# Output projection of the first ten token tiles in 64-row tiles, in pairs, between the transposed score tiles

## The chip, the cores and the metric

One core of a Trainium2 chip runs the whole program. The metric is the device time of one execution in microseconds (us). The engines are TensorE (PE, with its weight loads written PEld), VectorE (DVE), ScalarE (ACT), GpSimd (POOL) and SyncE (SP), which here only issues DMAs.

## What is computed

The input is x, 2048 tokens by 512 features, in float32. After a layer norm there are two branches: attention with 32 heads of 16 features, and a dense layer with GELU; the result joins them.

```python
xn = _layernorm(x)
q, k, v = (xn @ wqkv) split into 32 heads of 16
p = softmax(q @ k.T * 16 ** -0.5)
s = (p @ v) @ wo
g = silu(gelu(xn @ w1 + b1) @ w2 + b2)
out = x + s * g
```

The kernel keeps float32 accuracy by splitting each operand of a projection into a high and a low part in the PE's float32r format, and adding three products: high by high, high by low, low by high.

## The kernel before

**The stages.** The first 480 us hold the layer norm, the projections, the dense branch (its result g goes to DRAM, `g_d`) and part of the row maxima of the scores. Then comes the attention loop (lines 944 to 962): 513 steps, sixteen for each of 32 units. A unit `u` is four heads by 512 queries (`g, c = divmod(u, NCH)`); a step is one unit with one tile of 128 keys.

**A step.** `ORDER` (line 40) writes out the order of the work of one step on PE:

- T, four times (`t_one`, line 715): a transposed score tile, 128 keys by 512 queries, of one head. The contraction has 50 rows, which lie from row 0 or from row 64 of the array: `t_one(ua, ka, i % 2, 1 - i // 2)` gives the four T the row halves 1, 1, 0, 0. ACT takes the exponential of the tile into `PT` (line 724). Its four PSUM banks (`t_tile`) are used in turn, so each T waits for the exponential of the T four before it.
- S, X and Y (`s_op`, line 205): scores for the row maxima of later units, with 48 rows from row 0 or 64. DVE reduces each 128x512 tile (line 185). X and Y write the two halves of one bank from the two row halves of the array, one after the other: a no-op on POOL (line 217) waits for X, and Y waits for the no-op. Steps up to 491 have S, X and Y (`"TXSTTSTYV"`), later ones don't (`"TTTTV"`).
- V (`pv_step`, line 781): the product of the exponentials of the step before with the values, for four heads at once, in tiles of 128 rows by 32 columns.

After the sixteenth V of a unit, its sums are moved out of PSUM and divided by their denominators (`o_move`, `o_den`, `o_div`), through DRAM, to give `ot`.

**What hangs between them.** `at(n, f, ..., pos=i)` (line 897) puts a piece of other work into step n behind its T number i; without `pos` behind the last T, ahead of V. All engines take their work in this program order. For a token tile t (128 tokens), the output projection consists of

- `load_gx`: two DMAs on SP, g and x of the tile into `GX[t]`;
- `w_token` (`w_round`, line 850): ACT copies the tile's attention output into the high parts `oh`, POOL subtracts to get the low parts `ol`;
- `gate`: ACT takes a tanh, DVE multiplies, which makes silu(g) up to a factor;
- `w_mul`: per k (a block of 128 features, of four) three matmuls with 128 rows and 512 columns into one PSUM bank (`s_tile`, a ring of three banks);
- `w_out`: DVE multiplies the bank by the gate (`w_gate`, line 883), POOL adds x (line 888), SP writes it out (line 889).

Tiles 0 to 9 (`NW`) are dealt out from step 492 (`DONE`) on, one in two steps: two k in the first of them, two in the second, each time behind the fourth T:

```python
    for t in range(NW):
        n = DONE + 2 * t
        at(n - 4, load_gx, t)
        at(n - 2, w_token, t)
        at(n, w_mul, t, KS[:2])
        at(n, gate, t)
        at(n + 1, w_mul, t, KS[2:])
        at(n + 1, w_out, t, nc.gpsimd)
```

The other six tiles follow behind the loop (lines 963 to 985), as the last unit allows.

**A buffer.** The scratch tiles `gx`, `oh` and `ol` are rings of 4, 3 and 3 buffers. `home(KB)` is the place of the keys `kt0`, which are no longer used by then.

Of the kernel before, what the change touches and what calls it, by code (L numbers as in the profile page):

```python
# [8 lines left out]
F32 = mybir.dt.float32  # L9
F32R = mybir.dt.float32r  # L10
# [6 lines left out]
P = 128  # L17
S = 2048
D = 512
H = 32  # L20
DH = 16
KT = D // P
# [11 lines left out]
NW = 10  # L34
# [7 lines left out]
KB = 3  # L42
# [5 lines left out]
def fused(ctx: ExitStack, tc: tile.TileContext, x, wqk, wv, wo, w1, b1, w2, b2, out):  # L48
    nc = tc.nc
# [26 lines left out]
    def mm3(ps, lhs, rhs, first, last, then=None):  # L76
        n = 0
        for a, b in ((0, 0), (0, 1), (1, 0)):
            nc.tensor.matmul(ps, lhs[a], rhs[b], start=first and n == 0, stop=last and n == 2)  # L79
            n += 1  # L80
            if then:
                then()

    QS, QT, MX, NM, MH = {}, {}, {}, {}, {}
    SYNC = mybir.DependencyInfo(mybir.DependencyClass.Sync, mybir.DependencyReason.DATA)
# [5 lines left out]
    def s_tile(held=False):  # L91
        pool = s_ring.pop(0)
        if not held:
            s_ring.append(pool)
        return pool.tile([P, CH], F32, name="ps"), pool
# [29 lines left out]
    def slot(i, shape, dtype=F32):  # L125
        return big.tile(list(shape), dtype, name=f"slot{i}")
# [27 lines left out]
    done = {u: 0 for u in range(NU)}  # L154
# [148 lines left out]
    for j in range(len(pairs)):  # L303
        for h in range(2):
# [9 lines left out]
            n = 2 if nd < len(parts) and parts[nd][2] and ready - nd > room else 1  # L314
            n = max(n, need - 2 * (left - 1))
            while nd < ready and n > 0:
                c, f, k = parts[nd]
# [224 lines left out]
    s_when, put, row = [], [0], [0, 0]  # L542
# [217 lines left out]
    wb = ctx.enter_context(tc.tile_pool(name="work_b", bufs=2))  # L760
# [4 lines left out]
    wo_h = kp.tile([P, KT, D], F32R, name="wo_h")  # L765
    wo_l = kp.tile([P, KT, D], F32R, name="wo_l")

    WR = {}

    def load_wo(k):  # L770
        WR[k] = wb.tile([P, 2, D], F32, name="gx", bufs=4)[:, 0]
        nc.sync.dma_start(WR[k], wo[k * P:(k + 1) * P, :])

    def wo_high(k):
# [51 lines left out]
    GX, OTS, PW, homes = {}, {}, {}, {}  # L826

    def home(i):
        if i not in homes:
            homes[i] = (slot(i, (P, KT, D)) if i < KB else  # L830
                        keep_r.tile([P, 2 * KT, D], F32, name="kt0"))
        return homes[i]

    def load_gx(t):
        i = 2 * (t % NCH)
        if t < NW:
            GX[t] = wb.tile([P, 2, D], F32, name="gx", bufs=4)
        elif t < NT - NCH:
            GX[t] = home(KB)[:, i:i + 2]
        else:  # L840
            GX[t] = home(1 + i // KT)[:, i % KT:i % KT + 2]
        nc.sync.dma_start(GX[t][:, 0], g_d[t * P:(t + 1) * P, :])
        nc.sync.dma_start(GX[t][:, 1], x[t * P:(t + 1) * P, :])
# [4 lines left out]
        nc.vector.scalar_tensor_tensor(g, e, 1.0, g, op0=OP.add, op1=OP.mult)  # L848

    def w_round(blocks, src, lo):  # L850
        oh = wb.tile([P, KT, P], F32R, name="oh", bufs=3)
        ol = wb.tile([P, KT, P], F32R, name="ol", bufs=3)
        n = len(blocks)
        nc.scalar.activation(oh[:, :n], src, AF.Copy)
        lo.tensor_sub(ol[:, :n], src, oh[:, :n].bitcast(F32))
        for i, b in enumerate(blocks):
            OTS[b] = (oh[:, i], ol[:, i])

    def w_token(t):
        c, i = divmod(t, NCH)  # L860
        w_round([(t, k) for k in KS], ot[c][:, :, i * P:(i + 1) * P], nc.gpsimd)

    def w_chunk(k, lo):
        w_round([(t, k) for t in T3], ot[NCH - 1][:, k].rearrange("p (t s) -> p t s", s=P), lo)

    def cols(t):
        n = 2 if t == NT - 1 else 1
        return [slice(i * D // n, (i + 1) * D // n) for i in range(n)]

    def w_mul(t, ks, parts=(0, 1)):  # L870
        if t not in PW:
            PW[t] = [ps_t.tile([P, CH], F32, name="pst") if NW <= t < NT - NCH or i else
                     ps_m.tile([P, CH], F32, name="ps") if t == NT - 1 else s_tile()[0]
                     for i, cs in enumerate(cols(t))]
        for i, cs in enumerate(cols(t)):
            if i in parts:
                for k in ks:
                    mm3(PW[t][i][:, :cs.stop - cs.start], OTS[t, k], (wo_h[:, k, cs], wo_l[:, k, cs]),
                        k == 0, k == KT - 1)

    def w_gate(t, i=0):
        gx, cs = GX[t], cols(t)[i]
        nc.vector.scalar_tensor_tensor(gx[:, 0, cs], PW[t][i][:, :cs.stop - cs.start], 0.5, gx[:, 0, cs],
                                       op0=OP.mult, op1=OP.mult)
# [12 lines left out]
    def at(n, f, *a, pos=3):  # L897
        todo.setdefault((n, pos), []).append((f, a))

    KS = tuple(range(KT))  # L900
# [21 lines left out]
            at(16 * u + (31 if u < NU - 2 else 22), o_div, u, nc.gpsimd)  # L922
    T3 = range(NT - NCH, NT)
    late = range(NW, NT)
    for t in range(NW):
        n = DONE + 2 * t
        at(n - 4, load_gx, t)
        at(n - 2, w_token, t)
        at(n, w_mul, t, KS[:2])
        at(n, gate, t)  # L930
        at(n + 1, w_mul, t, KS[2:])
        at(n + 1, w_out, t, nc.gpsimd)
    for i, t in enumerate(late):
        n = L - 2 * len(late) - 1 + 2 * i
        at(n - 4, load_gx, t)
        at(n, gate, t)
    for i, t in enumerate(late[:2]):
        at(L - 2 + i, w_token, t)
    for k in range(KT):
        at(104 + 16 * k, load_wo, k)  # L940
        at(110 + 16 * k, wo_high, k)
        at(114 + 16 * k, wo_low, k)
    jobs.extend(heads[made[0]:])
    for n in range(L + 1):
        ua, ka = divmod(n, 16)
        want = due(n) - due(n - 1)
        i = 0
        for op in ORDER[want] if n > 1 else ("TTTTV", "TTSTSVT")[n]:
# [8 lines left out]
            else:  # L957
# [4 lines left out]
                i += 1  # L962
    o_move(NU - 1)
    w_mul(late[0], KS)
    w_chunk(0, nc.gpsimd)
    o_den(NU - 1)
# [52 lines left out]
```

## Time and profile before

| what | value |
|---|---|
| time, median of 3 runs | 1606.27 us (1606.13 to 1606.79) |
| profiled execution, span from first to last instruction | 1603.9 us |
| profiled execution, own time | not told apart from its span by the profile |
| PE busy | 1593.1 us (99%) |
| DVE busy | 1383.5 us (86%) |
| ACT busy | 1260.5 us (79%) |
| POOL busy | 377.5 us (24%) |
| mean granted PE clock | 1.000 |

The profile is of one execution. In a timeline each row gives the start in us from the span's start, the length, the engine, the line of the kernel, the operation, what it writes and reads, and how many were merged; in brackets how long the engine was idle before it and for whom it waited. A PE row's length holds the passage through the array: matmuls overlap, so the distance of their starts tells what one costs. "128*32 128x512" is a matmul with weights of 128 rows and 32 columns and a moving operand of 128 rows and 512 columns.

### The profile page before, as it was taken

The numbers are of one execution on the slowest core, as the hardware profiler recorded it, in microseconds if no ns is written. First come the engines' busy times: TensorE is split into PE (matmuls) and PEld (weight loads), VectorE is DVE, ScalarE is ACT, GpSimd is POOL, SyncE is SP. The second block draws the span as 40 slices with busy tenths as digits, with TensorE's granted clock in tenths as the row PEclk, the third lists the DMA queues.
The fourth block names the chain that finished last, engine by engine and source line by source line (L and its number), as shares of the span: only waits on it lengthen the run. The fifth ranks groups of instructions, "written<-read, shape, count | busy, mean of one in ns | idle before, by whom it ended". The sixth has DMA issues, their size and how long they took to land.

```text
span 1603.9 us, 32476 instructions
## 1 busy us (share of the span) xinstructions
PE 1593.1 (99%) x12146; PEld 915.7 (57%) x12146; DVE 1383.5 (86%) x2267; ACT 1260.5 (79%) x2524; POOL 377.5 (24%) x398
## 2 busy tenths in 40 slices
PE   8999999999999999999999999999999999999998
PEld 7899989999994444444444444444444444444445
DVE  7489888888989999999999999999999999999734
ACT  4333443434339999999999999999999999999984
POOL 4145565766640001011100200100010000000144
PEclk9999999999999999999999999999999999999999
DMA  6525343454322113111410411221141111110152
GB/s 204 149 59 151 116 136 97 148 145 126 114 89 70 40 30 70 29 36 42 79 32 27 68 42 29 59 42 29 30 70 30 30 29 37 34 29 22 58 200 91
DMA packets 76798, 116.93 MB, mean 73 GB/s; under 512 B 25156, under 2 KB 26436, under 8 KB 75464
## 3 DMA queue, kind: packets, MB, share of 16 engines
q1 hardware_dynamic: 73180, 102.42, 22.4%
q0 software_dynamic: 3264, 12.35, 3.9%
q8 instruction: 96, 1.57, 0.4%
q14 instruction: 62, 0.51, 0.1%
q10 hardware_dynamic: 196, 0.07, 0.0%
HBM read 84.35 MB, written 25.97 MB: 69 GB/s over the span
## 4 chain that ended last, share of the span: by engine, by line
PE 97%; DVE 1%; ACT 0%; DMA 0%; issue 0%; SPq 0%; DVEq 0%; ACTq 0%
PE pv L787 32%; PE ps L179 18%; PE pst L722 16%; PE ps L573 12%; PE pst L573 7%; PE ps L722 5%; PE ps L79 3%; PE pv L573 2%; PE pst L79 1%; DVE slot L74 0%; DMA xt<-in_x 0%; PE pst L259 0%; DVE st L407 0%; PE ps L259 0%; DVE xn L421 0%
## 5 line engine op out<-in xcount | busy, mean ns | idle before, releaser
L185 DVE TENSOR_REDUCE mx<-ps 128x2 f32<-128x512 f32 x2048 | 1299.4, 685 | 153.3 <-PE ps L179 84.9
L724 ACT ACTIVATE slot<-pst 128x512 f32<-128x512 f32 x1533 | 835.1, 612 | 14.2 <-PE pst L722 4.1
L787 PE MATMUL pv<-slot,vsb 128*32 128x512 f32 x4096 | 545.3, 605 | 0.0
L179 PE MATMUL ps<-kt,slot 48*128 48x512 f32 (+1 forms) x1364 | 393.1, 376 | 0.0
L722 PE MATMUL pst<-qt,kt 50*128 50x512 f32 x1149 | 378.1, 430 | 0.5 <-DVE gt L655 0.3
L722 PEld LDWEIGHTS pst<-qt,kt 50*128 50x128 f32 x1149 | 183.0, 184 | 249.6 <-ACT slot L724 246.2
L724 ACT ACTIVATE slot<-ps 128x512 f32<-128x512 f32 x515 | 314.8, 612 | 12.9 <-PE pst L722 8.2
L179 PEld LDWEIGHTS ps<-kt,slot 48*128 48x128 f32 x1364 | 211.3, 184 | 34.2 <-DVE mx L185 23.3
L573 PE MATMUL ps<-slot,w1h 64*128 64x512 f32 x1088 | 220.5, 394 | 0.0
L179 PE MATMUL ps<-kt,qz 48*128 48x512 f32 x512 | 214.9, 420 | 0.0
L179 PE MATMUL ps<-slot,slot 48*128 48x512 f32 (+1 forms) x598 | 172.6, 376 | 0.0
L722 PE MATMUL ps<-qt,kt 50*128 50x512 f32 x387 | 163.0, 423 | 0.0
L573 PEld LDWEIGHTS ps<-slot,w1h 64*128 64x128 f32 x1088 | 152.9, 185 | 6.8 <-ACT junk L587 0.8
L787 PEld LDWEIGHTS pv<-slot,vsb 128*32 128x32 f32 x4096 | 80.6, 108 | 119.8 <-issue 112.0
L573 PE MATMUL ps<-slot,w1l 64*128 64x512 f32 x544 | 143.0, 392 | 0.0
L367 POOL TENSOR_TENSOR hl<-hg,hh 128x512 fp32r<-128x512 f32 x76 | 96.8, 1296 | 131.7 <-ACT hh L366 95.0
L722 PE MATMUL pst<-qt,slot 50*128 50x512 f32 x384 | 119.8, 424 | 0.0
L587 ACT ACTIVATE junk<-ident_r 1x1 f32<-1x1 f32 x92 | 18.0, 196 | 126.4 <-PE pst L573 123.2
L722 PEld LDWEIGHTS ps<-qt,kt 50*128 50x128 f32 x387 | 71.1, 184 | 69.4 <-ACT slot L724 56.5
L179 PEld LDWEIGHTS ps<-kt,qz 48*128 48x128 f32 x512 | 93.7, 183 | 17.4 <-DVE mx L185 0.6
L243 POOL CAST nmh<-nm 128x16 fp32r<-128x16 f32 x32 | 6.3, 197 | 413.1 <-PE pst L722 209.1
L722 PEld LDWEIGHTS pst<-qt,slot 50*128 50x128 f32 x384 | 61.5, 184 | 71.9 <-ACT slot L724 71.6
(150 smaller groups left out, 1744.9 us busy)
## 6 DMA issues: line engine op xcount, KB each, us to landing
raw<-in_w SPq DMA_DIRECT2D x88, 256.0 KB
qk_h<-hh SPq DMA_DIRECT2D x32, 256.0 KB
qk_l<-hl SPq DMA_DIRECT2D x32, 256.0 KB
qt<-qk_h SPq DMA_DIRECT2D x128, 64.0 KB
slot<-qk_h SPq DMA_DIRECT2D x92, 64.0 KB
xt<-in_x SPq DMA_DIRECT2D x16, 256.0 KB
g_d<-gt POOLq DMA_DIRECT2D x16, 256.0 KB, 3.1
qt<-qk_l SPq DMA_DIRECT2D x64, 64.0 KB
```

Of the source, the lines that this page charges most:

```text
L79: nc.tensor.matmul(ps, lhs[a], rhs[b], start=first and n == 0, stop=last and n == 2)
L179: return nc.tensor.matmul(ps[:, c0:c0 + w], QS[u][r, p, qi * P:(qi + 1) * P], kts[u // NCH % KB][p][r, k0:k0 + w], start=True, stop=True).ins
L185: nc.vector.tensor_reduce(MX[u][:, 2 * p:2 * p + 2, qi, ki][:, heads, parts], ps.rearrange("p (n c) -> p n c", c=HC), axis=AX.X, op=OP.max)
L243: nc.gpsimd.tensor_copy(hl[:, 0], nm)
L367: nc.gpsimd.tensor_sub(hl, raw, hh.bitcast(F32))
L573: i = nc.tensor.matmul(ps, lhs[r], rhs[r], start=first, stop=last).ins
L587: i = nc.scalar.activation(junk[:, :1], ident_r[:1, :1].bitcast(F32), AF.Copy).ins
L722: nc.tensor.matmul(ps, kts[g % KB][p][r, k * P:(k + 1) * P], QT[u][r, p, :], start=True, stop=True)
L724: nc.scalar.activation(PT[u, k][:, 2 * p + a, :], ps, AF.Exp, scale=SCALE)
L787: nc.tensor.matmul(PV[u][32 * j:32 * j + 32, :], vsb[:, k, h:h + 32], PT[u, k][:, j, :], start=(k == 0), stop=(k == NT - 1))
```

## The change

Tiles 0 to 9 are now taken in pairs (t, t + 1), each pair in four steps. Each 128-row matmul becomes two of 64 rows. In the first two steps of a pair, tile t takes rows 0 to 63 of all four k and tile t + 1 rows 64 to 127; in the last two the tiles swap row halves (`side`). Per step and pair there are twelve 64-row matmuls, alternating between row half 0 and 1: four each behind the first, the second and the third T. A no-op on POOL waits for the last matmul ahead of the swap, and the first two behind it wait for the no-op. `w_out` of both tiles stands in the pair's last step. Tile t + 1's `w_token` moves to the first T of the step before the pair; the loads stand three and two steps ahead of the pair. The ring of `gx` has three buffers and those of `oh` and `ol` four; tiles 3 and 7 use the place of `kt0`.

```diff
     def load_wo(k):
-        WR[k] = wb.tile([P, 2, D], F32, name="gx", bufs=4)[:, 0]
+        WR[k] = wb.tile([P, 2, D], F32, name="gx", bufs=3)[:, 0]
...
-        if t < NW:
-            GX[t] = wb.tile([P, 2, D], F32, name="gx", bufs=4)
+        if t < NW and i < 6:
+            GX[t] = wb.tile([P, 2, D], F32, name="gx", bufs=3)
         elif t < NT - NCH:
-            GX[t] = home(KB)[:, i:i + 2]
+            GX[t] = home(KB)[:, i - 6 * (t < NW):][:, :2]
...
-        oh = wb.tile([P, KT, P], F32R, name="oh", bufs=3)
-        ol = wb.tile([P, KT, P], F32R, name="ol", bufs=3)
+        oh = wb.tile([P, KT, P], F32R, name="oh", bufs=4)
+        ol = wb.tile([P, KT, P], F32R, name="ol", bufs=4)
...
+    turned = {}
+
+    def w_half(t, part, third):
+        two = (t, t + 1)
+        if part == 0 and third == 0:
+            for b in two:
+                PW[b] = [s_tile()[0]]
+        side, ks = divmod(part, 2)
+        ops = [(k, i, j) for k in KS[2 * ks:2 * ks + 2] for i, j in ((0, 0), (0, 1), (1, 0))]
+        for n in (2 * third, 2 * third + 1):
+            for a in range(2):
+                b, r, (k, i, j) = two[a ^ side], slice(64 * a, 64 * a + 64), ops[n]
+                op = nc.tensor.matmul(PW[b][0], OTS[b, k][i][r], (wo_h, wo_l)[j][r, k], start=part == 0 and n == 0,
+                                      stop=part == 3 and n == 5).ins
+                if part == 2 and n == 0:
+                    tc.add_manual_dep(op, turned[t].name, SYNC, reason="other row tile")
+        if part == 1 and third == 2:
+            turned[t] = nc.gpsimd.nop().ins
+            tc.add_manual_dep(turned[t], op.name, SYNC, reason="row tile done")
...
-    for t in range(NW):
+    for t in range(0, NW, 2):
         n = DONE + 2 * t
-        at(n - 4, load_gx, t)
-        at(n - 2, w_token, t)
-        at(n, w_mul, t, KS[:2])
-        at(n, gate, t)
-        at(n + 1, w_mul, t, KS[2:])
-        at(n + 1, w_out, t, nc.gpsimd)
+        for b in range(2):
+            at(n - 3 + b, load_gx, t + b)
+            at(n - 2 + b, w_token, t + b, pos=3 * (1 - b))
+            at(n + b, gate, t + b)
+        for part in range(4):
+            for third in range(3):
+                at(n + part, w_half, t, part, third, pos=third)
+        for b in range(2):
+            at(n + 3, w_out, t + b, nc.gpsimd)
```

## The prediction

> **What bounds the kernel now.** I read the page first, then TensorE's timeline of the stretch that the change touches, then the other engines' timelines there.
>
> ```profile
> span 1603.9 us, 32476 instructions
> PE 1593.1 (99%) x12146; PEld 915.7 (57%) x12146; DVE 1383.5 (86%) x2267; ACT 1260.5 (79%) x2524; POOL 377.5 (24%) x398
> PE 97%; DVE 1%; ACT 0%; DMA 0%; issue 0%; SPq 0%; DVEq 0%; ACTq 0%
> ```
>
> The chain that ended last is TensorE (PE) nearly throughout, so time that the change takes from PE shortens the end, unless another engine then becomes late. One step of the touched stretch on PE (the PE timeline; columns: start, length, what):
>
> ```profile
> 1527.14 1.06 PE L787 MATMUL pv<-slot,vsb 128*32 128x512 f32 x8
> 1528.13 0.50 PE L722 MATMUL ps<-qt,kt 50*128 50x512 f32 x1
> 1528.14 0.72 PE L722 MATMUL pst<-qt,kt 50*128 50x512 f32 x3
> 1528.79 0.50 PE L79 MATMUL ps<-wo_h,oh 128*128 128x512 f32 x1
> 1529.13 0.39 PE L79 MATMUL ps<-wo_l,oh 128*128 128x512 f32 x1
> ...
> 1530.05 0.39 PE L79 MATMUL ps<-wo_h,ol 128*128 128x512 f32 x1
> 1530.37 0.64 PE L787 MATMUL pv<-slot,vsb 128*32 128x512 f32 x4
> ```
>
> A step is V (1.0 us: 1527.14 to 1528.13), T (four score tiles, 0.66 to 1528.79) and W (six 128-row matmuls, 1.58 to the next V). W is dear at its ends: the first matmul holds the array 0.34, the last 0.32 before V starts; the four between take 0.23 each. From T to W and from W to V the array changes its tiling.
>
> The whole stretch, by the starts of V in step 491 (the last with row-maximum work), 492, 493 and 511:
>
> ```profile
> 1513.39 1.06 PE L787 MATMUL pv<-slot,vsb 128*32 128x512 f32 x8
> 1517.00 1.07 PE L787 MATMUL pv<-slot,vsb 128*32 128x512 f32 x8
> 1518.00 0.25 PE L259 MATMUL pst<-ident_r,nmh 128*32 128x128 f32 x1
> 1518.17 0.50 PE L722 MATMUL ps<-qt,kt 50*128 50x512 f32 x1
> 1520.63 1.07 PE L787 MATMUL pv<-slot,vsb 128*32 128x512 f32 x8
> 1579.08 1.92 PE L787 MATMUL pv<-slot,vsb 128*32 128x512 f32 x16
> ```
>
> From 1513.39 to 1579.08 are 65.69 us: step 492 3.61, step 493 3.63 (with the transposition of the last row maxima, 0.17 before T), then 18 of 3.25 on average.
>
> **The change on PE, step by step.** Removed per step: six 128-row matmuls behind T. Added: twelve 64-row matmuls in front of the second, third and fourth T, alternating between the row halves. T uses 50 rows from row 0 or 64, so T and W now share one tiling, and one of three changes of tiling per step goes. Each half then has eight matmuls a step (half 1: two T, six W; half 0 the same).
>
> The trace has 64-row matmuls on both halves before the attention (PE timeline; then a row of the windows view: length, PE busy and its matmuls; then the page's weight loads):
>
> ```profile
> 59.72 0.39 PE L573 MATMUL pv<-kt,slot 64*128 64x512 f32 x1
> 59.73 0.39 PE L573 MATMUL pst<-kt,slot 64*128 64x512 f32 x1
> 59.95 0.39 PE L573 MATMUL pv<-kt,slot 64*128 64x512 f32 x1
> ```
> ```profile
> 300.00:350.00 50.00, 50.00 (x419) 1.00 0.47 137
> ```
> ```profile
> L573 PEld LDWEIGHTS ps<-slot,w1h 64*128 64x128 f32 x1088 | 152.9, 185 | 6.8 <-ACT junk L587 0.8
> ```
>
> Two matmuls start together and the next pair 0.23 later: call this a slot. With 48-row score matmuls mixed in, 419 in 50 us make 0.239 a slot. Weight loads are doubled by the change (twelve for six), but two of 0.185 per slot of 0.23 are hidden in this stretch already, since the halves load side by side. That is the cover; I cost them at nothing. Mixing 48 and 64 rows costs no change of tiling either. The first slot behind V is longer, as in a step with score work on both halves:
>
> ```profile
> 1505.71 0.50 PE L722 MATMUL pst<-qt,kt 50*128 50x512 f32 x1
> 1506.05 0.39 PE L722 MATMUL ps<-qt,kt 50*128 50x512 f32 x1
> ```
>
> So a new step is V 1.0 + first slot 0.34 + six at 0.233 (1.40; bounds 0.23 and 0.239, taken near the purer row) + last start to V 0.32 (taken from W's row above) = 3.06, rounded down to 3.05 because V to T reads 0.99. Bounds: 3.03 and 3.10. Against 3.25 that is 0.20 a step.
>
> This needs each half to run its own queue, for the program order of halves in a step is 1 0 1 0 1 1 0 1 0 1 0 0 1 0 1 0. The T rows say that it does. The four T are issued to halves 1, 1, 0, 0 (line 959), yet a second one starts 0.01 behind the first (1528.13, 1528.14), and W, which needs both halves free, starts after 0.66: two slots (0.34 + 0.32), not three.
>
> [...]
>
> **What it moves: a new wait in step 491.** The second tile's rounding (ACT copy L854, POOL subtraction L855) goes from step 492 to the first T of step 491. There a POOL no-op (L217), which releases the last row-maximum matmul Y, is queued behind it. Before (timelines of ACT and of all engines):
>
> ```profile
> 1512.32 0.65 ACT L854 ACTIVATE oh<-slot 128x512 fp32r<-128x512 f32 x1
> 1512.84 0.62 ACT L724 ACTIVATE slot<-pst 128x512 f32<-128x512 f32 x1
> ```
> ```profile
> 1513.05 1.28 POOL L855 TENSOR_TENSOR ol<-slot,oh 128x512 fp32r<-128x512 f32 x1 [23.96 <-ACT oh L854]
> 1513.08 0.18 PEld L179 LDWEIGHTS ps<-kt,slot 48*128 48x128 f32 x1 [0.39 <-POOLq L217]
> ```
>
> Y already waits for the no-op behind the first tile's subtraction, and is released as soon as that is handed to POOL. With the change the second copy stands behind the exponential of 1512.84: it starts 0.5 later at 1513.3, ends 0.65 later at 1514.0, POOL then takes its subtraction, and Y starts at about 1514.1 instead of 1513.08. V and all PE work are behind Y: **+1.0 us**, once. If the no-op must also wait for the first subtraction to end (1514.33), it is 1.35; the lower end is 0, were the subtraction handed over unwaited. I take 1.0, since Y's weights loaded 0.03 after the first subtraction started, not after it ended. Part is given back: ACT catches up meanwhile, so step 492 no longer needs 3.61.
>
> **The sum.** 65.69 before; after: 1.0 + 20 x 3.05 + 0.17 (the transposition) = 62.17. Gain 3.5 us. Bounds: 20 x 3.03 without the stall gains 4.9, 20 x 3.10 with 1.35 gains 2.2.
>
> **What lies beside it.** ACT:
>
> ```profile
> 1569.55 0.65 ACT L847 ACTIVATE slot<-gx 128x512 f32<-128x512 f32 x1
> 1570.06 0.65 ACT L854 ACTIVATE oh<-ot 128x512 fp32r<-128x512 f32 x1
> 1570.87 0.60 ACT L724 ACTIVATE slot<-ps 128x512 f32<-128x512 f32 x1 [0.16 <-PE pst L722]
> 1571.37 1.57 ACT L724 ACTIVATE slot<-pst 128x512 f32<-128x512 f32 x3
> 1572.80 0.65 ACT L847 ACTIVATE slot<-slot 128x512 f32<-128x512 f32 x1
> ```
>
> Four exponentials take 1.93 (1570.87 to 1572.80), every other operation 0.51; four steps hold 16 exponentials and at most six others: 10.8, 2.7 a step, under 3.05. T3 now comes last instead of before W; its exponential ends about 0.8 after V starts, before the next V needs it.
>
> The last steps, POOL, SP and DVE (timeline):
>
> ```profile
> 1579.18 0.69 DVE L883 SCALAR_TENSOR_TENSOR gx<-ps,gx 128x512 f32<-128x512 f32 x1 [1.70 <-PE ps L79]
> 1579.95 1.28 POOL L888 TENSOR_TENSOR gx<-gx 128x512 f32<-128x512 f32 x1 [1.33 <-DVE gx L883]
> 1581.19 1.28 POOL L855 TENSOR_TENSOR ol<-ot,oh 128x512 fp32r<-128x512 f32 x1
> 1581.94 1.15 SPq L810 DMA_DIRECT2D ot<-os  x2
> 1584.29 0.39 PE L79 MATMUL pst<-wo_h,ol 128*128 128x512 f32 x1
> 1584.34 0.33 SPq L816 DMA_DIRECT2D den_d<-dr  x1
> ```
>
> Two gates and two additions now stand at a pair's end. The first gate frees its bank 0.8 after V starts (1579.87 in the old time); the next pair writes that bank 1.3 after (behind V and the first slot). In step 511 the extra addition puts the last subtraction back by 1.28, to 1583.75, still 0.5 before the matmul that reads it (1584.29). SP holds its queue for the second output until about 1582.6, so the two moves of 1581.94 end near 1584.1, before the denominators at 1584.34. Both are nothing, with half a microsecond of cover. The swap's no-op stands on POOL behind the two additions of the previous pair, which end 3.4 after the V before the pair; it is wanted two steps (6.1) after: hidden. With three gx buffers a load waits on SP for the output of three loads back, issued two steps earlier, while the gate that wants it is three steps off: hidden. The last row maxima go through DRAM:
>
> ```profile
> 1518.59 0.32 SPq L268 DMA_DIRECT2D mh_d<-mh  x1
> 1521.68 1.36 SPq L150 DMA_DIRECT2D qt<-mh_d  x2
> ```
>
> They are issued by 1523.04 and wanted by T at 1528.13; the stall and shorter steps take some 1.5 of these 5.
>
> The end behind step 511 is untouched, so span 1603.9 becomes 1600.4. The profile gives no time of its own execution beside the span; the median 1606.27 lies 2.4 above it, which I leave as it is: **1602.8 us**.
>
> **Rivals.**
> *Strict order.* If PE starts matmuls only in program order, the two same-half neighbours in the order above cost a ninth slot: step 3.28, sum 1.0 + 65.6 + 0.17, 1.1 slower: 1607.4. If those two also bare their weight loads (0.34 less 0.233 each), 4.3 more: 1611.7, clearly **slower**. It decides from the first blocked T on, the second of each step. Against it: the T rows. Chance 0.13.
> *ACT sets the step.* If ACT's order leaves it the idle half microsecond a step that it has now (3.25 less 2.7), a step shrinks only to 3.2: 1.0 + 64.0 + 0.17 = 65.2, a gain of 0.5: 1605.8. Against it: the 2.7 above. Chance 0.08.
> *The swap waits.* If the no-op is held on POOL by one operation of 1.28 at each of five swaps, 6.4 us more than forecast: 1609.2. Against it: POOL is idle by then. Chance 0.03.
> *No stall in step 491*: 1601.8. Chance 0.06.
> My own case, eight slots and the stall, has 0.70, spread over 1601.4 to 1604.1.
>
> **Chances.** A measurement of this kernel tells about 0.2% (3.2 us, 1603.06) from no change. My case lies on that bound: 0.45 of its 0.70 below it, 0.25 above. Faster 0.45 + 0.06 = 0.51; within 0.2%: 0.25 + 0.08 + 0.05 (strict order with loads hidden) = 0.38; slower 0.08 + 0.03 = 0.11. Range 1601.4 to 1606.0, leaving out strict order and the late swap.
>
> **What would show it.** Right: V to V 3.05 in steps 494 to 511, W pairs 0.01 apart on PE, Y some 1.0 later behind L217. Wrong: V to V of 3.28 with T alone in its slot; PE waiting for ACT between T; a wait on a POOL no-op every fourth step; the tail behind step 511 longer than the 24.8 from 1579.08 to the span's end.

## The result and the profile after

The changed kernel takes 1602.73 us (median of 9 runs, 1602.18 to 1605.09) against 1606.13 (9 runs) on the same chip: a ratio of 0.9979, with a 95% interval of 0.9970 to 0.9989. 1602.8 had been forecast, with a range of 1601.4 to 1606.0. The page after:

```profile
span 1600.4 us, 32720 instructions
PE 1588.7 (99%) x12266; PEld 916.2 (57%) x12266; DVE 1377.7 (86%) x2267; ACT 1262.1 (79%) x2524; POOL 378.2 (24%) x398
PE 97%; DVE 1%; ACT 0%; DMA 0%; issue 0%; POOL 0%; SPq 0%; DVEq 0%; ACTq 0%
```

The span is 3.5 us shorter, PE holds the chain as before (97% of it), and its busy time fell by 4.4. One new step on PE (timeline of the changed kernel; L893 is the new 64-row matmul):

```profile
1523.57 1.06 PE L787 MATMUL pv<-slot,vsb 128*32 128x512 f32 x8
1524.57 0.50 PE L722 MATMUL ps<-qt,kt 50*128 50x512 f32 x1
1524.57 0.73 PE L893 MATMUL ps<-wo_h,oh 64*128 64x512 f32 x2
1524.90 0.39 PE L893 MATMUL ps<-wo_l,oh 64*128 64x512 f32 x1
...
1526.30 0.39 PE L893 MATMUL ps<-wo_h,ol 64*128 64x512 f32 x1
1526.30 0.39 PE L722 MATMUL pst<-qt,kt 50*128 50x512 f32 x1
1526.62 0.64 PE L787 MATMUL pv<-slot,vsb 128*32 128x512 f32 x4
```

The first score tile and the first projection matmul start together, the last of both start together 1.73 later, and the next V starts 0.32 after them: eight slots and V in 3.05, where the old step took 3.25. The starts of V over the stretch, with Y of step 491:

```profile
1510.81 1.06 PE L787 MATMUL pv<-slot,vsb 128*32 128x512 f32 x8
...
1513.91 0.39 PE L179 MATMUL ps<-kt,slot 48*128 48x256 f32 x1 [1.01 <-POOLq L217]
1514.23 1.06 PE L787 MATMUL pv<-slot,vsb 128*32 128x512 f32 x8
...
1517.28 1.07 PE L787 MATMUL pv<-slot,vsb 128*32 128x512 f32 x8
1518.28 0.25 PE L259 MATMUL pst<-ident_r,nmh 128*32 128x128 f32 x1
...
1520.51 1.07 PE L787 MATMUL pv<-slot,vsb 128*32 128x512 f32 x8
```
```profile
1575.57 1.92 PE L787 MATMUL pv<-slot,vsb 128*32 128x512 f32 x16
```

The bracket behind Y is the new wait: PE stands 1.01 for POOL's no-op. Step 492 takes 3.05, step 493 with the transposition 3.23, the next 18 a mean of 3.06 (55.06 from 1520.51). What holds the no-op (ACT, then POOL):

```profile
1512.67 0.62 ACT L724 ACTIVATE slot<-pst 128x512 f32<-128x512 f32 x1
1513.14 0.66 ACT L854 ACTIVATE oh<-slot 128x512 fp32r<-128x512 f32 x1
```
```profile
1512.88 2.50 POOL L855 TENSOR_TENSOR ol<-slot,oh 128x512 fp32r<-128x512 f32 x2 [23.96 <-ACT oh L854]
```

The second copy ends at 1513.80, POOL's record of the no-op stands at 1513.8, and Y starts at 1513.91, all while the first subtraction runs (1512.88 to 1514.15, 1.27) and the second has not started. So the no-op, which the program puts behind both, came with the end of the copy that the second one needs, and before either had ended.

### The profile page after: what moved, and what is told of

Read it like the earlier page. It is cut to its first block, busy times and chain, and to the rows that moved or that the text cites. A ratio compares the mean times of both kernels' runs of the same rounds, so it can differ in the third digit from the quotient of the medians.

```text
span 1600.4 us, 32720 instructions
## 1 busy us (share of the span) xinstructions
PE 1588.7 (99%) x12266; PEld 916.2 (57%) x12266; DVE 1377.7 (86%) x2267; ACT 1262.1 (79%) x2524; POOL 378.2 (24%) x398
## 4 chain that ended last, share of the span: by engine, by line
PE 97%; DVE 1%; ACT 0%; DMA 0%; issue 0%; POOL 0%; SPq 0%; DVEq 0%; ACTq 0%
PE pv L787 32%; PE ps L179 18%; PE pst L722 16%; PE ps L573 12%; PE pst L573 7%; PE ps L722 5%; PE pv L573 2%; PE ps L79 2%; PE ps L893 1%; PE pst L79 1%; DVE slot L74 0%; ACT slot L724 0%; DMA xt<-in_x 0%; DVE st L407 0%; PE pst L259 0%
## 5 line engine op out<-in xcount | busy, mean ns | idle before, releaser
L722 PE MATMUL pst<-qt,kt 50*128 50x512 f32 x1149 | 383.8, 428 | 0.6 <-DVE gt L655 0.4
L722 PEld LDWEIGHTS pst<-qt,kt 50*128 50x128 f32 x1149 | 187.8, 184 | 250.5 <-ACT slot L724 245.8
```

The source lines that it names most:

```text
L722: nc.tensor.matmul(ps, kts[g % KB][p][r, k * P:(k + 1) * P], QT[u][r, p, :], start=True, stop=True)
```

## Experiments

The theory (A): the matmuls between two changes of the array's tiling (a group) cost PE about 0.20 beyond their slots (0.34 for the first and 0.32 for the last, less two slots of 0.23); the 64-row matmuls share the score tiles' tiling, so one change less in each of 20 steps is the gain; each row half has a queue of its own; the moved rounding costs 1.0 once. Rivals: dealing the matmuls among the score tiles feeds ACT better (B); the schedule in pairs is what gains (C). All edits are to the changed kernel. e2, e4, e6 and e7 are one execution each. Spans differ by up to a microsecond in the work ahead of step 489, which no edit but e9's touches, so I compare distances between starts of V ("V to V").

**e1: 64-row matmuls, not dealt.**

```diff
-                at(n + part, w_half, t, part, third, pos=third)
+                at(n + part, w_half, t, part, third, pos=3)
```

> All twelve 64-row matmuls of a step stand behind its fourth score tile; nothing else differs from the changed kernel. Theory A (one tiling change less per step, each row half with its own queue: eight slots wherever the matmuls stand): V to V stays 3.06, span about 1600.4. Rival B (the gain comes from dealing the matmuls between the score tiles, which feeds ACT more evenly): V to V goes back to 3.25, span about 1604.2.

Measured: V to V 3.06, ratio to the kernel before 0.9983 (0.9974 to 0.9993). B falls. Only step 493 got longer, 3.82 instead of 3.23 (timeline of e1):

```profile
1518.59 0.50 PE L722 MATMUL ps<-qt,kt 50*128 50x512 f32 x1
1518.59 1.33 PE L722 MATMUL pst<-qt,kt 50*128 50x512 f32 x3
1519.43 0.18 PEld L722 LDWEIGHTS pst<-qt,kt 50*128 50x128 f32 x1 [0.55 <-DVE mh L267]
1519.44 0.72 PE L893 MATMUL ps<-wo_h,oh 64*128 64x512 f32 x2
```

The last score tile of that step waits until DVE has read the transposed maxima out of its bank (0.55, the bracket on its weight load), and the projection matmuls behind it wait along (the first starts at 1519.44). Dealt, that tile comes late enough: the changed kernel shows no such wait, and 3.23 for the step. So dealing is worth 0.6 us in one step and nothing in the others.

**e3: the pairs' schedule with the old 128-row matmuls.**

```diff
+        b = two[side]
...
-            for a in range(2):
-                b, r, (k, i, j) = two[a ^ side], slice(64 * a, 64 * a + 64), ops[n]
-                op = nc.tensor.matmul(PW[b][0], OTS[b, k][i][r], (wo_h, wo_l)[j][r, k], start=part == 0 and n == 0,
-                                      stop=part == 3 and n == 5).ins
...
+            k, i, j = ops[n]
+            nc.tensor.matmul(PW[b][0], OTS[b, k][i], (wo_h, wo_l)[j][:, k], start=ks == 0 and n == 0,
+                             stop=ks == 1 and n == 5)
...
-                at(n + part, w_half, t, part, third, pos=third)
+                at(n + part, w_half, t, part, third, pos=3)
```

> The pairs' schedule of the changed kernel, but with the old 128-row matmuls (six a step, tile t in the first two steps of a pair, tile t + 1 in the last two, no swap), behind the fourth score tile. Theory A: the tiling change is back, V to V 3.25, and the wait in step 491 stays: 1.0 + 0.17 + 20 x 3.25 = 66.2 against 65.7 before, span about 1604.4, a little slower than the kernel before. Rival C (the gain comes from the pairs' schedule: loads, gates and outputs at other places): V to V 3.06, span about 1600.4.

Measured: V to V 3.25, step 491 3.41, ratio 1.0004 (0.9995 to 1.0014). From V of step 490 to that of 511 it takes 68.96, where the kernel before takes 68.10 and the changed one 64.76. C falls: the schedule alone gains nothing. In e1 and e3 the projection matmuls stand at the same place, and T and W fill eight slots a step; what differs is the tiling of W, and 0.19 a step with it.

**e2: 128-row matmuls, dealt** (as e3, without the edit of its last two lines).

> As e3, but with the six 128-row matmuls dealt in twos behind the first three score tiles. Theory A: every group between two tiling changes costs its matmuls at 0.23 and 0.20 besides (0.34 first and 0.32 last instead of 0.23 each); four groups of one score tile (0.43) and three of two matmuls (0.66) make 3.7, with V 4.7 a step, 29 more than e3: span about 1634. Rival B: no longer than 3.25 a step, span 1604 or less.

Measured: V to V 4.69, span 1633.3. One step on PE:

```profile
1542.95 1.07 PE L787 MATMUL pv<-slot,vsb 128*32 128x512 f32 x8
1543.95 0.49 PE L722 MATMUL ps<-qt,kt 50*128 50x512 f32 x1
1544.37 0.51 PE L893 MATMUL ps<-wo_h,oh 128*128 128x512 f32 x1
...
1545.04 0.50 PE L722 MATMUL pst<-qt,kt 50*128 50x512 f32 x1
...
1547.64 1.06 PE L787 MATMUL pv<-slot,vsb 128*32 128x512 f32 x8
```

A score tile alone holds the array 0.42, two matmuls 0.67: each time 0.2 above their slots of 0.23. Against e3 there are five more groups (1.0) and the four score tiles no longer run two by two (two slots, 0.46): 1.46, measured 1.44. So in this run too a group costs 0.2, at a place where that had not been read, and where no V stands beside the change.

**e4: the halves in blocks instead of alternating**, behind the fourth score tile.

```diff
-        if part == 0 and third == 0:
+        if part == 0:
...
-        for n in (2 * third, 2 * third + 1):
-            for a in range(2):
+        for a in range(2):
+            for n in range(6):
...
-            for third in range(3):
-                at(n + part, w_half, t, part, third, pos=third)
+            at(n + part, w_half, t, part, 2)
```

> As e1, but the twelve 64-row matmuls of a step are issued as six of half 0 and then six of half 1, instead of alternating. Theory A with a queue for each half: the two blocks still run side by side, V to V 3.06, span about 1600.4. Strict order of starts: half 1 idles through half 0's block, fourteen slots instead of eight, V to V about 4.5, span about 1628. A look-ahead of a few matmuls only: between the two.

Measured: V to V 3.64, between the 3.06 of independent halves and the 4.5 of strict order. One step on PE (the L893 rows up to 1564.90 are all of half 0):

```profile
1563.86 0.49 PE L722 MATMUL ps<-qt,kt 50*128 50x512 f32 x1
1563.87 0.72 PE L722 MATMUL pst<-qt,kt 50*128 50x512 f32 x3
1564.43 0.40 PE L893 MATMUL ps<-wo_h,oh 64*128 64x512 f32 x1
1564.67 0.39 PE L893 MATMUL ps<-wo_l,oh 64*128 64x512 f32 x1
1564.90 0.39 PE L893 MATMUL ps<-wo_h,ol 64*128 64x512 f32 x1
1564.91 0.61 PE L893 MATMUL ps<-wo_h,oh 64*128 64x512 f32 x2
...
1566.18 0.39 PE L893 MATMUL ps<-wo_h,ol 64*128 64x512 f32 x1
1566.50 1.06 PE L787 MATMUL pv<-slot,vsb 128*32 128x512 f32 x8
```

Half 0 runs alone for two slots; half 1's first matmul starts beside half 0's third, past three that were issued ahead of it and had not started. Then both run until half 0 is done, and half 1 ends alone. All this costs 0.58, of which the lead is 0.48 (1564.43 to 1564.91). So in this step PE started a matmul of one half past waiting ones of the other, past three of them and not more. The order of the change asks it to overtake two at most. That each half has a queue, and a short one, is my reading of these starts; no run shows the queues themselves. A strict order of starts is not what this run did: for it 4.5 a step was expected above, and it took 3.64.

**e5: no wait in step 491.** For the first pair, ACT copies at the end of steps 489 and 490, POOL subtracts at the end of 490 and 491.

```diff
+        low = lambda: lo.tensor_sub(ol[:, :n], src, oh[:, :n].bitcast(F32))
+        if blocks[0][0] < 2:
+            LOW[blocks[0][0]] = low
...
+            if t == 0:
+                at(n - 3 + b, w_token, b)
+                at(n - 2 + b, lambda b: LOW.pop(b)(), b)
...
```

> For the first pair alone, each tile's high part is copied by ACT one step before its low part is subtracted by POOL (copies at the end of steps 489 and 490, subtractions at the end of 490 and 491), so that no row-maximum no-op stands on POOL behind a subtraction that waits for ACT. Theory A (the no-op behind the subtraction costs the 1.0 in step 491): V of step 491 to that of 490 falls from 3.42 to 2.1 or 2.2, span about 1599.1. Rival D (PE would wait for the late ACT there in any case): under 0.3 gained, span 1600.1 or more.

Measured: step 491 2.39 instead of 3.42; ratio 0.9976 (0.9967 to 0.9985). The span was 1600.0, since 0.6 were lost ahead of step 490. Run again beside the changed kernel on one chip:

> The kernel e5 once more, for the comparison on the same chip with e10 and with the changed kernel: span 1599 to 1600 by e5, and the changed kernel 1.0 more from step 490 on.

> The changed kernel once more, on the same chip as e5 and e10: span about 1600.4 to 1601; the ratio to the kernel before 0.998.

The changed kernel came to 0.9980 (0.9971 to 0.9989), span 1600.4, step 491 3.41; e5 to 0.9970 (0.9959 to 0.9982), span 1599.6, step 491 2.40. A gain of 1.0 in that step, as A says; D falls. The two intervals overlap; the step's distance is what shows it. Timelines of PE (with its weight loads) and of POOL in the second run of e5:

```profile
1512.99 0.18 PEld L722 LDWEIGHTS pst<-qt,kt 50*128 50x128 f32 x1 [0.30 <-ACT slot L724]
1513.00 0.38 PE L179 MATMUL ps<-kt,slot 48*128 48x256 f32 x1
1513.41 1.07 PE L787 MATMUL pv<-slot,vsb 128*32 128x512 f32 x8
```
```profile
1511.06 1.29 POOL L857 TENSOR_TENSOR ol<-slot,oh 128x512 fp32r<-128x512 f32 x1 [21.95 <-PE pst L722]
1513.53 1.28 POOL L857 TENSOR_TENSOR ol<-slot,oh 128x512 fp32r<-128x512 f32 x1 [1.18 <-PE pst L722]
```

Y no longer waits for an ACT copy (it starts 0.01 behind the last score tile's weight load), and 2.39 is still not the 2.1 that I expected. The kernel before has 2.41 there, but for another reason: in it Y waits 0.39 for the no-op; in e5 the last score tile waits 0.30 for an exponential, since ACT had made a copy ahead of it. So PE does wait for a late ACT there, as D has it, but for 0.3 and not for the 1.0.

**e6: three swaps per pair.**

```diff
-        side, ks = divmod(part, 2)
+        ks, side = divmod(part, 2)
...
-                if part == 2 and n == 0:
+                if part > 0 and n == 0:
...
-        if part == 1 and third == 2:
+        if part < 3 and third == 2:
```

> The tiles of a pair swap row halves after each of their four steps instead of once: three no-ops and waits per pair instead of one. Theory A (V lies between the halves' last use and the next, and hides the no-op): V to V stays 3.06, span about 1600.4. Rival E (each swap holds PE for a no-op's way, some 0.3 to 0.4 as where Y waits for X in the old stretch): ten more swaps, 3 to 4 us more, span about 1604.

Measured: V to V 3.06 throughout, span 1600.5. E falls: with V (1.0) in between, the ten more swaps cost nothing that the 3.06 or the span shows.

**e7: four of the twelve matmuls.** It leaves out the eight that use a low part; all four k stay, other than the expectation says ("half of the projection's k").

> Leaves out eight of the twelve 64-row matmuls of each step (the low parts, and half of the projection's k), to see what bounds the step behind PE. Theory A: PE needs 1.0 + 0.34 + 2 x 0.23 + 0.32 = 2.1, so ACT's 2.7 sets the step: span about 1593. If ACT is already the bound at 3.06: no change, 1600.4. If ACT overlaps better than counted: down to 2.1 a step, span about 1581.

Measured: steps of 2.1 to 3.9, a mean of 2.75 over the 20 (55.05 from V of step 491 to that of 511). ACT is busy for 95% of it (windows, up to the last V: length, then PE, PEld, DVE, ACT, POOL busy):

```profile
1515.13:1571.73 56.60, 53.57 (x330) 21.70 (x329) 21.53 (x30) 54.01 (x109) 27.44 (x23) 1.00 0.55 184
```

Half of ACT's 2.6 of idle time are two waits for a load of g (0.81 and 0.53). So 2.75 is what a step takes where ACT sets it, close to the 2.7 counted, and the changed kernel stands 0.3 above it. The span fell to 1596.1 only, not to 1593: 0.9 was lost before V of step 491, the 20 steps took 1.0 more than at 2.7 each, and the end got 1.1 longer, 0.7 of it a last V that waits for ACT.

**e8: V in twos**, from step 492 on, on top of e5.

```diff
-                if n:
-                    pv_step(*divmod(n - 1, 16))
+                for m in () if n == 0 else (n - 1,) if n <= 492 else () if n % 2 else (n - 2, n - 1):
+                    pv_step(*divmod(m, 16))
```

> e5, and from step 492 on V is issued in twos: none in odd steps, those of two steps in even ones. A test of the same price at another place: it takes away one more pair of tiling changes in two steps. Theory A: two steps hold sixteen slots in one run (0.34 + 14 x 0.233 + 0.32 = 3.92) and two V in one run (0.88 + 1.0), 5.80 for two against 6.12, some 2.9 less over the stretch, as far as ACT's 2.75 a step lets it: span about 1597 (1597 to 1598.5). Rival: the first and last slot's excess isn't the tiling change but the first use of new data after V, or ACT holds T back: no gain, 1600.

Measured: two steps take 6.13 and 6.68 by turns instead of the 5.80 expected, ratio 0.9991 (0.9982 to 1.0000), worse than e5. The timeline has waits at the two places where no V stands any more, the swap and the next pair's first matmul:

```profile
1532.88 0.19 PEld L897 LDWEIGHTS ps<-wo_h,oh 64*128 64x128 f32 x2 [0.31 <-POOLq L902]
```
```profile
1539.78 0.47 PE L897 MATMUL ps<-wo_h,oh 64*128 64x512 f32 x1 [0.64 <-DVE gx L907]
```

V had covered both, as the prediction says of the bank and the expectation of e6 of the swap: in the changed kernel, where V stands at both places, PE has neither wait from 1514 to 1576.

**e10: V in twos at the ends of odd steps**, which puts them at both borders.

```diff
+                for m in () if n == 0 else (n - 1,) if n <= 493 or n == L else () if n % 2 == 0 else (n - 2, n - 1):
...
-            at(16 * u + 17, o_move, u, pos=0)
+            at(16 * u + (17 if u < NU - 2 else 18), o_move, u, pos=0)
```

(and `o_den`, `o_div` of that unit one step later).

> As e8, but the two V stand at the end of the odd steps, so that they lie at both borders of a pair's halves (the swap and the change of pair), and the last unit but one is moved out one step later. Theory A with the waits seen in e8 (0.31 for the swap's no-op, 0.64 and a bare first slot for the gate's bank, at the borders that had no V): these are hidden again, two steps take 5.8 instead of 6.13, span about 1597. Rival: what was lost in e8 was lost to ACT's uneven supply and not to these waits: 1600 or more.

Measured: two steps 5.78 (5.80 expected), ratio 0.9962 (0.9949 to 0.9976), the fastest version: 1599.79 us, against 1601.21 for e5 and 1602.35 for the changed kernel on the same chip. So e8's loss lay in its two waits and not in ACT's supply. The rows of PE:

```profile
1530.42 1.06 PE L787 MATMUL pv<-slot,vsb 128*32 128x512 f32 x8
1532.84 1.06 PE L787 MATMUL pv<-slot,vsb 128*32 128x512 f32 x8 [1.36 <-ACT os L794]
1537.77 1.92 PE L787 MATMUL pv<-slot,vsb 128*32 128x512 f32 x16
1543.56 1.92 PE L787 MATMUL pv<-slot,vsb 128*32 128x512 f32 x16
```

The span is 1598.1, not the 1597 expected. One wait is new, and longer than what is missing: at a unit's border the second V needs the one bank that holds the sums of the first, and ACT must empty it before (1.36).

**e9: V in twos in the whole loop**, on top of e8.

```diff
-                for m in () if n == 0 else (n - 1,) if n <= 492 else () if n % 2 else (n - 2, n - 1):
+                for m in () if n == 0 else (n - 1,) if n <= 2 else () if n % 2 else (n - 2, n - 1):
```

> e8 with V in twos in the whole attention loop, also in the 490 steps with row-maximum work. Theory A for PE alone: 0.16 less a step than 2.07, 1.91; but DVE's three reductions take 1.95 and ACT's four exponentials 1.93 a step, so at most 0.1 a step: span 1550 to 1590. Rival: DVE and ACT, at 94%, can't follow the uneven order, and PE waits for them at once: 1597 or more.

Measured: 13% slower, ratio 1.1291 (1.1276 to 1.1307), span 1814.7, where 1550 to 1590 was expected: the side of the rival, and far beyond it. While two V run, ACT and DVE run dry (0.97 and 1.23 idle), and PE waits for DVE afterwards (0.21):

```profile
800.51 1.92 PE L787 MATMUL pv<-slot,vsb 128*32 128x512 f32 x16
...
802.89 1.09 ACT L724 ACTIVATE slot<-pst 128x512 f32<-128x512 f32 x2 [0.97 <-PE pst L722]
...
803.02 3.17 DVE L185 TENSOR_REDUCE mx<-ps 128x2 f32<-128x512 f32 x5 [1.23 <-PE ps L179]
...
804.36 0.49 PE L179 MATMUL ps<-kt,slot 48*128 48x512 f32 x1 [0.21 <-DVE mx L185]
```

How much of the loss is this and how much the order of the row-maximum tiles was not separated.

## Why the prediction held, point by point

- **The step.** 3.06 against 3.05; the first slot 0.33, the rest 0.233 on average (1.40 for six), the last 0.32. The slot was taken near the purer of two rows, and that was right.
- **Own queues.** The starts are as forecast from them in this order (eight slots and V in 3.05); in e4 a matmul passed three of the other half and not more, and its 3.64 is not the 4.5 of strict order. The queues themselves are inferred, here and in the prediction.
- **The wait in step 491.** 1.0 forecast; Y starts 3.10 after V of step 490 instead of 2.10. e5 confirms the cause.
- **The transposition** cost 0.18 (0.17). Step 492 gave back its old excess, as said.
- **ACT.** 2.7 counted, 2.75 measured in e7, where it sets the step.
- **The tail.** From V of step 511 to the span's end it is 24.8, before and after:

```profile
1575.68 1.29 DVE L903 SCALAR_TENSOR_TENSOR gx<-ps,gx 128x512 f32<-128x512 f32 x2 [3.57 <-PE ps L893]
1576.51 2.52 POOL L908 TENSOR_TENSOR gx<-gx 128x512 f32<-128x512 f32 x2 [1.34 <-DVE gx L903]
...
1578.99 1.30 POOL L855 TENSOR_TENSOR ol<-ot,oh 128x512 fp32r<-128x512 f32 x1
1579.48 1.15 SPq L810 DMA_DIRECT2D ot<-os  x2
1580.79 0.39 PE L79 MATMUL pst<-wo_h,ol 128*128 128x512 f32 x1
1581.27 0.33 SPq L816 DMA_DIRECT2D den_d<-dr  x1
```

  The last subtraction ends 0.5 before its reader, as worked out. One step was a little off: the denominators were to leave 5.26 after V of step 511 as before, and left 5.70 after it: not behind SP's queue, which was free by 1580.63, but because the reciprocal came 2.55 after the issue of its DMA instead of 2.12. It cost nothing, as the end shows.
- **What was luck.** The stretch itself gained 3.34 (from V of step 490 to that of 511: 68.10 before, 64.76 after), not 3.5. What is missing is the step rounded down: with the 3.06 of the sum the forecast of the stretch would have been 3.3. The other 0.17 were gained ahead of step 490, where the kernels are alike and single executions differ by more. Luck too is the 2.4 left between span and median: where the runs list both, a time stands 1.7 to 1.9 above its own span; the rest is that the profiled execution was some 0.6 faster than the median, after and, worked out the same way, before. The measured gain of 3.4 is clear of no change, but at 0.21% it lies right at the 0.2% that the prediction named, as its chances allowed for.

## What to carry to other kernels

Where matmuls of two tilings alternate, count the groups as well as the matmuls: here a group of score or projection matmuls cost 0.20 us beyond its slots, and one of V 0.15 (1.00 alone, 1.85 two together in e10). Here projection matmuls that took the tiling of the score tiles cost their slots alone: 0.19 less a step (3.06 in e1, 3.25 in e3). Before moving work, look for what is queued behind its waits on every engine (the no-op on POOL: 1.0), and for what a long block of other work hides: V hid a swap and a bank's release, and moving V uncovered both (0.31 and 0.64 in e8). Leaving work out measures where the next engine sets the step: here ACT, at 2.75 in e7.

## What the runs showed of the hardware

Both points are read from the starts of instructions in this case's profiles; how the engines queue their work inside was not measured.

- PE, row halves: in the step of e4 shown above, a matmul of half 1 started at 1564.91, beside the third of half 0's six (1564.90) and ahead of the other three, which were issued before it. In the orders 1 1 0 0 (kernel before: two slots, 0.66) and 1 0 1 0 1 1 0 1 0 1 0 0 1 0 1 0 (changed kernel: eight slots, 2.05) the halves lost no slot to each other.
- POOL, a no-op behind two subtractions: in the changed kernel it is recorded at 1513.8, with the end of the copy that the second subtraction needs (1513.80) and before the end of the first subtraction (1514.15), and Y, released by it, started at 1513.91. In the kernel before, Y's weights loaded at 1513.08, 0.03 after the start of the one subtraction ahead of its no-op, which took 1.28.
